# Fillers that follow the token loads, and a second hand-written issue order, in an adaLN block with local attention and a token-mixing MLP

## The chip, the cores and the metric

The kernel runs on one core of a Trainium2 chip. A core has five engines, each with its own instruction queue that is worked off in order: TensorE (PE in the profile, the matrix engine; its weight loads are shown as PEld), VectorE (DVE), ScalarE (ACT), GpSimd (POOL) and SyncE (SP), which here only issues DMA transfers. The engines wait for one another by semaphores. Matrix results land in PSUM, everything else lies in SBUF.

The metric is the time of one execution on the device, in microseconds (us). The kernel before takes 198.67 us, the median of three runs (198.6, 198.67 and 198.73). Smaller is better.

## What is computed

One block of 2048 tokens of 512 features. A vector c gives six modulation rows (shift, scale and gate for two halves). The first half is attention with 32 heads of 16 features, in which each token sees eight tokens: itself and those 2, 4, ... 14 places back. The second half is an MLP that mixes tokens, not features: w1 is 2048 x 1792 and takes the sum over all tokens. Cut to what matters:

```
mod = silu(c) @ w_mod                       # sa, ca, ga, sb, cb, gb
h = layernorm(x) * (1 + ca) + sa
q, k, v = h @ wqkv                          # 32 heads of 16
logits[s, w] = q[s] . k[s - 2w] / 4         # w = 0..7, masked where s - 2w < 0
x = x + ga * (softmax(logits) @ v[s - 2w]) @ wo
h = layernorm(layernorm(x) * (1 + cb) + sb)
u = gelu(einsum("sd,sf->df", h, w1) + b1)   # sum over all 2048 tokens
x = x + gb * (einsum("df,fs->ds", u, w2) + b2).T
```

## The kernel before, in words

Tokens lie in 16 tiles of 128. They are worked in five chunks of 2, 4, 4, 4 and 2 tiles (chunk 0 is tiles 0 and 1, chunk 1 tiles 2 to 5, and so on). Each step of the work is an operation with a name, built by a Python graph (`_Graph.add_any`). Many have alternatives on several engines. The order in which the operations are written out, and so the order of each engine's queue, is a table by hand or by a planner outside the file: the string `ORDER` (line 180 on). A name in it may carry a letter: `:a`, `:d`, `:p` choose ACT, DVE or POOL, `:s` skips the operation, and `:q` writes a matmul as four column tiles of 32 instead of one of 128. Without a letter the first alternative holds. `schedule` also gives out buffers in that order: six PSUM banks (`ps`), four product buffers (`big`), five buffers for shifted v (`vd`).

The names that the change and the prediction speak of:

- `ld_x*`, `ld_wmod*`, `ld_wqkv*`, `ld_wo*`, `ld_w1_*`, `ld_w2_*`, `ld_row*`: loads, issued from SP. `ld_wmod1` and `ld_wmod0` bring the scale and the shift of the first half.
- `ident`, `halo0`, `consts`: constants made on GpSimd. `cps` transposes c; `silu_exp`, `silu_dve` make silu(c); `modcols1` and `modcols0` (line 553 on) are 32 small matmuls that make the scale and the shift as columns; `a1col` and `sab` copy them out of PSUM.
- `ln1s*`, `ln1v*`, `rstd1_*`, `rste1_*`, `nb1_*`, `n1_*`: statistics and normalization of tiles for chunk 0 to 4. Statistics are one pass on DVE or two on ACT (`:a`).
- `tr0_0`, `tr1_0`, `tr1_2` transpose chunks 0 and 1 on PE; `hT0_0` to `hT0_3` and `hT1_*` take them out of PSUM and multiply by `a1col`. The four of chunk 0 read one PSUM bank. Chunks 2 to 4 are transposed by DMA (`xt6` to `xt15`, on SP), and their weights are scaled instead (`wsc0_*`, `wsc1_*`, `wsc2_*`).
- `qvb0`, `qvb1`, `qkv<chunk>_<which><group>`, `ev*`: projections to q (0), k (1) and v (2), and their way out of PSUM.
- `qk*`: the products of q and shifted k, on DVE, into `big`; `red*` sums them over features on PE in column tiles; `max`, `sub`, `exp`, `esum`, `rcp`, `rcq`, `smB` are the softmax. `a2_*` and `vd*` are DMA copies of the weights and of shifted v; `pv*` are the second products on DVE and `pvacc*` their sums on PE, again in column tiles; `oev*` copies them out.
- `wo*`, `x1_*`: output projection and residual. Where `x1_*` runs on ACT, PE adds the residual with a fifth matmul; where it runs on DVE, PE makes four.
- `ln2*`, `n2_*`, `aff*`, `afb*`, `ln3*`, `h3_*`: the two layernorms of the second half, tile by tile. `n2` and `h3` may run on ACT, DVE or GpSimd. `aff` and `afb` of a group of tiles (0, 2, 6, 10, 12, 14, 15) read all the `n2` of the group.
- `mlp1_<part>_<row block>_<first tile>`: the token sum with w1. As soon as some tiles of `h3` are ready, PE can work on their share; partial sums are parked (`park`, `padd`). The weights come through a ring of three buffers (`wst`). `gelu*`, then `mlp2_*` with w2, `fin*` on DVE and the stores `st_out*` from SP or ACT.
- `warm*` (line 523 on): fillers, matmuls on the identity whose result nobody reads. `warm0` is twelve of them, placed by the dependence `wmA1` between `cps` and `modcols`. Seven more blocks of two exist; the table skips six, and `warm1` stands at the very end.

All operations are written by one helper, so every row of the profile has line 131; rows are told apart by their tiles (`big`, `hT`, `wst` and so on).

Of the kernel before, what the change touches and what calls it, by code (L numbers as in the profile page):

```python
# [186 lines left out]
ev0_12 ln1v12 ln1v13 wsc1_1:a qkv0_22 qk0_1 qkv1_13 ld_wmod2 ld_wo3 qk0_0 qk0_2 n1_8 red0_0 red0_1 ln1s11:a qkv1_03:q  # L187
qvb_cp1 qk0_3 xt6 red0_2 ld_wmod3 ev1_13 ev1_03 red0_3 mask wsc2_3:a ln1v11 ln1s10 ld_b1 ld_wo0 xt8 ev0_20 xt7 qkv1_11
ev1_11 ln1v10 max0 qkv1_01 ev1_01 rstd1_3 ev0_22 qk1_3 xt9 sub0 exp0 qkv1_00 ev1_00 qkv1_10 ev1_10 wsc1_0:a vd0_0
qk1_1 qkv1_02 esum0 rcp0 wsc0_2:p qk1_0 ev1_02 qkv1_12 qkv1_23 ld_wmod4 ld_wmod5 rcq0 ev1_12 qkv1_21 rste1_3 smB0  # L190
# [838 lines left out]
```

## Time and profile before

| | |
|---|---|
| runs | 198.6, 198.67, 198.73 us |
| span of the profiled execution | 196.8 us, from its first to its last instruction; no time of its own is listed beside it, the median stands 1.9 above it |
| granted TensorE clock | 0.999 on average |
| PE busy | 185.2 us (94%), 1850 matmuls |
| DVE busy | 156.6 us (80%) |
| ACT busy | 124.9 us (63%) |
| POOL busy | 19.9 us (10%) |
| HBM | 22.03 MB read, 2.10 MB written |

In a row of the profile the numbers after an operation are the count and the busy time or duration; a bracket tells how long the engine stood idle before it, and what ended that. A row in order of time begins with its start and its length. PE rows overlap, since matmuls are pipelined: the pace is read from start to start. The chain that ended last is followed back from the last instruction, each step to what released it.

### The profile page before, as it was taken

The numbers are of one execution on the slowest core, as the hardware profiler recorded it, in microseconds if no ns is written. First come the engines' busy times: TensorE is split into PE (matmuls) and PEld (weight loads), VectorE is DVE, ScalarE is ACT, GpSimd is POOL, SyncE is SP. The second block draws the span as 40 slices with busy tenths as digits, with TensorE's granted clock in tenths as the row PEclk, the third lists the DMA queues.
The fourth block names the chain that finished last, engine by engine and source line by source line (L and its number), as shares of the span: only waits on it lengthen the run. The fifth ranks groups of instructions, "written<-read, shape, count | busy, mean of one in ns | idle before, by whom it ended". The sixth has DMA issues, their size and how long they took to land.

```text
span 196.8 us, 4628 instructions
## 1 busy us (share of the span) xinstructions
PE 185.2 (94%) x1850; PEld 95.5 (48%) x1867; DVE 156.6 (80%) x244; ACT 124.9 (63%) x293; POOL 19.9 (10%) x38
## 2 busy tenths in 40 slices
PE   0699999999999999899999999999999999999994
PEld 0369554654444467244544454444444444444453
DVE  2888999999999999999999999965841633453664
ACT  6877999998999999999797889812760000000000
POOL 5123006320000005030000031200000000000000
PEclk9999999999999999999999999999999999999999
DMA  5998478778899732969674768888939293001112
GB/s 169 312 366 248 115 165 256 235 216 238 165 193 317 252 131 80 312 167 249 199 200 136 159 176 180 197 250 170 336 65 309 82 257 102 30 27 53 53 53 82
DMA packets 55369, 35.95 MB, mean 183 GB/s; under 512 B 24628, under 2 KB 52788, under 8 KB 55348
## 3 DMA queue, kind: packets, MB, share of 16 engines
q1 hardware_dynamic: 53468, 34.05, 63.2%
q10 hardware_dynamic: 1880, 1.61, 2.5%
q8 instruction: 14, 0.23, 0.5%
q14 instruction: 7, 0.06, 0.1%
HBM read 22.03 MB, written 2.10 MB: 123 GB/s over the span
## 4 chain that ended last, share of the span: by engine, by line
PE 73%; DVE 13%; ACT 5%; issue 3%; DMA 2%; SPq 1%; POOL 0%; DVEq 0%; ACTq 0%
PE psS L131 71%; DVE big L131 9%; DVE h L131 2%; PE psL L131 2%; ACT junk L131 1%; SPq L131 1%; DMA vD<-v_sb 1%; ACT xx L131 1%; DMA xx<-in_A_x_dram 1%; DVE m L131 1%; ACT o_sb L131 1%; ACT lsb L131 0%; DVE mv L131 0%; POOL h L131 0%; ACT v_sb L131 0%
## 5 line engine op out<-in xcount | busy, mean ns | idle before, releaser
L131 PEld LDWEIGHTS <-wst 128*128 128x128 bf16 (+1 forms) x566 | 35.5, 100 | 31.9 <-issue 1.3
L131 PE MATMUL psS<-h,wst 128*32 128x512 bf16 (+1 forms) x400 | 50.5, 379 | 0.4 <-issue 0.3
L131 DVE TENSOR_TENSOR big<-q_sb,k_f 128x4096 bf16<-128x4096 bf16 (+1 forms) x20 | 36.4, 1857 | 0.5 <-ACT k_f L131 0.5
L131 DVE TENSOR_TENSOR big<-a2sb,vD 128x4096 bf16<-128x4096 bf16 (+1 forms) x20 | 36.6, 1858 | 0.0
L131 DVE SCALAR_TENSOR_TENSOR h<-psS,bcol,rows_bc 128x512 f32<-128x512 f32 (+2 forms) x18 | 12.4, 690 | 24.2 <-PE psS L131 24.0
L131 PE MATMUL psS<-hT,w_qkv 128*32 128x512 bf16 (+3 forms) x414 | 28.7, 337 | 0.8 <-ACT v_sb L131 0.4
L131 PEld LDWEIGHTS <-w_qkv 128*32 128x32 bf16 (+1 forms) x462 | 19.9, 108 | 16.4 <-issue 2.7
L131 PE MATMUL psS<-gT,big 128*128 128x512 bf16 x109 | 24.3, 379 | 0.2
L131 POOL TENSOR_SCALAR h<-xx,rs,nb 128x512 bf16<-128x512 bf16 x6 | 10.6, 1777 | 84.2 <-DVE nb L131 84.2
L131 PEld LDWEIGHTS <-big 128*128 128x128 bf16 x144 | 12.0, 98 | 13.7 <-issue 0.5
L131 ACT ACTIVATE junk<-xx 128x512 bf16<-128x512 bf16 x28 | 17.7, 631 | 1.3 <-DVE xx L131 0.3
L131 ACT ACTIVATE h<-xx,nb,rs 128x512 bf16<-128x512 bf16 x22 | 17.2, 818 | 0.4 <-DVE nb L131 0.4
L131 PE MATMUL psS<-woq,o_sb 128*32 128x512 bf16 (+1 forms) x123 | 15.8, 380 | 0.4 <-ACT o_sb L131 0.4
L131 ACT ACTIVATE gT<-psS,bcol 128x512 bf16<-128x512 f32 x14 | 8.8, 686 | 10.6 <-DVE psS L131 10.6
L131 DVE TENSOR_TENSOR psS<-psS,gT 128x512 f32<-128x512 f32 x14 | 9.2, 695 | 6.3 <-PE psS L131 6.3
L131 DVE TENSOR_TENSOR h<-h,xx 128x512 bf16<-128x512 f32 (+2 forms) x18 | 11.4, 633 | 0.7
L131 ACT ACTIVATE q_sb<-psS,qvb 128x512 bf16<-128x512 f32 (+1 forms) x20 | 11.6, 603 | 0.3 <-PE psS L131 0.2
L131 PEld LDWEIGHTS <-group 128*32 128x32 bf16 x288 | 7.0, 96 | 9.8 <-issue 4.0
L131 PE MATMUL psS<-hT,wst 128*128 128x256 bf16 (+2 forms) x74 | 11.3, 333 | 0.1
L131 ACT ACTIVATE v_sb<-psS,qvb 128x512 bf16<-128x512 f32 (+1 forms) x20 | 11.2, 607 | 0.0
L131 DVE TENSOR_TENSOR h<-h,rows_bc 128x1024 bf16<-128x1024 bf16 (+2 forms) x14 | 10.5, 759 | 0.0
L131 ACT ACTIVATE k_f<-psS 128x512 bf16<-128x512 f32 x16 | 9.7, 606 | 1.1 <-PE psS L131 1.1
(90 smaller groups left out, 223.3 us busy)
## 6 DMA issues: line engine op xcount, KB each, us to landing
vD<-v_sb SPq DMA_DIRECT2D x12, 524.5 KB, 4.8
big<-in_B_w_dram SPq DMA_DIRECT2D x4, 896.0 KB, 7.5
vD<-v_sb SPq DMA_DIRECT2D x8, 268.5 KB, 3.1
wst<-in_B_w_dram SPq DMA_DIRECT2D x3, 640.0 KB, 5.4
xx<-in_A_x_dram SPq DMA_DIRECT2D x7, 256.0 KB, 5.6
wst<-in_B_w_dram SPq DMA_DIRECT2D x2, 800.0 KB, 4.7
gT<-in_w_mod_dram SPq DMA_DIRECT2D x3, 512.0 KB, 5.4
wst<-in_B_w_dram SPq DMA_DIRECT2D x2, 768.0 KB, 5.6
```

Source lines behind the costliest of these rows:

```text
L131: r = fn(*a, **k)
```

## The change

Two things are changed together.

The fillers: eight blocks of 1, 3, 8, 1, 1, 3, 2 and 1 matmuls (`WARM`). A second tuple, `GATE`, gives five of them a tile of tokens as the moving operand in place of the identity: blocks 2 to 6 multiply tiles 1, 8, 2, 4 and 6, and so cannot run before that tile is loaded. None is skipped. `warm0` loses its place between `cps` and `modcols` (the dependence `wmA1` is gone), and the table places all eight: on PE the order at the beginning becomes `cps`, `warm0`, `warm1`, `warm7`, `warm3`, `warm4`, `warm2`, `warm6`, `modcols1`, `tr0_0`, `warm5`, `modcols0`, `tr1_0`, `tr1_2`, `qvb0`, `qkv0_00`, `qkv0_10`, `qkv0_02`. Before it was `cps`, `tr0_0`, `warm0`, `modcols1`, `modcols0`, `tr1_2`, `tr1_0`, `qvb0`, `qkv0_00`, `qkv0_02`, `qkv0_10`.

The table: the same 805 names in another order, and with other letters at 99 of them. On GpSimd the operations are now `ident`, `halo0`, `consts`, `n1_1`, `n1_0`, `n1_5`, `n1_7`, `n1_6`, `n1_9`, `wsc1_3`, `wsc1_2`, `n1_8`, `n1_10`, `n2_1`, `halo_v2`, `n2_5`, `h3_1`, `h3_0`, `halo_v4`, `n2_8`, `n2_13`, `h3_10`, `h3_13`, `h3_12`; before they were `halo0`, `ident`, `consts`, `n1_0`, `wsc0_1`, `wsc1_2`, `wsc0_3`, `wsc0_2`, `n1_13`, `halo_v2`, `n2_5`, `h3_0`, `h3_1`, `n2_12`, `n2_13`, `n2_15`, `h3_11`. Of the transposes of chunk 0, three of four evacuations go from DVE to ACT, of chunk 1 two of three. `:q` stands at 37 names instead of 48. Written one behind the other, PE's operations change between column-tiled ones (`red`, `pvacc`, `mask`, `modrow` and those with `:q`) and whole ones 26 times before and 16 times now. `esum4` goes from PE to DVE, `x1_10` from ACT to DVE. Behind its last `pvacc4`, PE had `mlp1_0_11_2`, `wo15`, `wo14`, `mlp1_0_13_0`, `mlp1_0_13_2`, `mlp1_0_11_6` and `mlp1_0_13_6` left of the parts before `mlp1_1` (18 matmuls with w1); now it has `mlp1_0_12_6`, `wo14`, `wo15`, `mlp1_0_13_0`, `mlp1_0_13_2` and `mlp1_0_13_6` (14). On SP `vd0_0` now stands between `a2_0_1` and `a2_0_2`, and `ld_w1_1_1408` behind `ld_w1_2_640`, no longer ahead of `ld_w1_2_0`; between `mlp1_1_9_10`, the last reader of the buffer that `ld_w1_2_640` fills, and `mlp1_1_11_10`, which needs `ld_w1_1_1408`, stand 35 matmuls.

```diff
@@ -178,60 +178,60 @@
 ORDER = """
-halo0 ident ld_c act_table cps silu_exp ld_x1 ld_x0 ln1s0 ln1v0 ln1s1:a ln1v1 rstd1_0 rste1_0 ld_x_2_8 ld_x_1_2 nb1_0
-consts ln1s9 silu_dve n1_1 n1_0:p tr0_0 ln1s8 ld_x_1_4 ln1s4:a ld_x_2_6 ln1s3:a warm0 ln1s5 ln1s7 ld_wmod1 ln1v5
-ld_wmod0 modcols1 modcols0 ln1v9 ln1v8 ln1v4 ln1s2 ln1v2 ld_wqkv0 ln1v7 ln1v3 ln1s6 ln1v6 rstd1_1 rste1_1 nb1_1 n1_4:d
-rstd1_2 rste1_2 n1_2:d n1_5:d nb1_2 ld_wqkv1 n1_3 n1_7 n1_6:d a1col hT0_2:d n1_9 tr1_2 tr1_0 hT1_1 wsc0_1:p hT0_1:d
-sab hT0_0:d ld_x_3_12 hT0_3:d hT1_3:d qvb0 qvb_cp0 qkv0_00 warm6:s wsc1_3:a hT1_2:d qkv0_02 ev0_00 ld_wqkv2 qkv0_10
-qkv0_12 ld_b2 ev0_10 ld_x_4_14 wsc1_2:p qkv0_20 wsc0_0 qvb1 ld_x_3_10 wsc0_3:p hT1_0:d ev0_02 wsc2_2:a ln1s13 ln1s12
...
-wo13 ln3s6 vd4_1 ln3v9 ln3v6 ln3s7 wo12 x1_10 ln2m10 ln3v7 mlp1_0_9_0 ln2q11 x1_12:d mlp1_0_9_2 ln2q10 a2_4_0 ln2w10
...
-ld_w1_1_896 h3_11:p mlp1_1_7_10 padd1_7 gelu7 padd1_4 padd1_5 mlp1_1_8_10 mlp1_1_10_10 padd1_10 ld_w1_1_1408 padd1_6
...
-fin15_0 st_out15_0 mlp2_15_2 mlp2_15_1 fin15_2 fin15_1 st_out15_1 st_out15_2:a warm1
+ident halo0 ld_c cps act_table silu_exp silu_dve ld_x1 ln1s1 warm0 ld_x0 ln1s0 ln1v0 ln1v1 rstd1_0 ld_x_2_8 ld_x_1_2
+ld_x_1_4 ld_x_2_6 ld_wmod1 ln1s2 ln1s3 warm1 rste1_0 consts nb1_0 ln1v2 warm7 ln1s8:a ln1s5 ln1v8 ln1v3 ld_wmod0 warm3
+ln1v5 ln1s4 warm4 warm2 ln1s9:a ln1v9 warm6 ln1s7 ln1v4 ld_wqkv0 rstd1_1 modcols1 ln1s6 ld_wqkv1 n1_1:p rste1_1 nb1_1
+n1_0:p n1_4 ln1v7 tr0_0 ln1v6 n1_3:d a1col warm5 modcols0 rstd1_2 n1_2:d n1_5:p tr1_0 rste1_2 nb1_2 ld_x_3_12 ld_wqkv2
+tr1_2 n1_7:p sab qvb0 ld_b2 hT0_3 ld_x_4_14 hT0_1 n1_6:p hT0_0:d ld_x_3_10 hT0_2 ld_wmod2 hT1_2 hT1_1 qkv0_00 wsc1_1:a
+wsc0_2 hT1_0 qkv0_10 qkv0_02 qkv0_12 wsc0_0 ev0_10 hT1_3:d qvb_cp0 ev0_00:d qkv0_20 qkv0_22 ln1s13 ld_wo3 n1_9:p
+wsc0_1:a xt6 ev0_02 ld_wmod5 ln1s12 qkv1_03 qk0_0 qvb1 ev0_12 wsc1_0:a wsc1_3:p qkv1_13 qk0_1 red0_0 qk0_3 red0_1
...
+qkv1_00 ln1s10:a ln1v15 ev0_20 ev1_11 n1_8:p ln1v13 qk1_3 ln1v11 xt8 xt7 qkv1_10 qkv1_23 xt9 max0 ln1v10 sub0 ev1_01
...
+qkv1_20 a2_0_2 a2_0_0 rste1_4 ld_wo2 vd0_2 halo_v1:a ev1_22 vd0_3 biascols sub1 vd0_1 ev1_21 qkv2_03 pv0_0 pvacc0_0
...
+qkv3_13 ev3_02 n2_1:p aff0 xt14 pv1_0 ev3_11 qkv3_00 halo_v2 afb0 ev3_01 pv1_1 sub2 exp2 pvacc1_0 ev3_00 oev1_0
...
+qk4_2 ln2q7 ln2q8 mlp1_0_1_2:q red4_2 mlp1_0_3_0:q vd3_1 ln2m6 park0_1 qk4_3 pv3_0 mlp1_0_2_2:q ln2w6 halo_v4 rstd2_6
...
+mlp1_0_6_0:q oev3_0 mlp1_0_7_2:q mlp1_0_6_2:q pvacc3_2 n2_8:p mlp1_0_5_0:q mlp1_0_5_2:q oev3_2 pvacc3_1 max4 pv3_3
...
+esum4:d rcp4 ld_w1_0_1408 wo13 park0_6 wo12 afb6 rcq4 x1_13:d smB4 wo11 a2_4_2 wo10 x1_12:d x1_11:d ln3s7:a ln3s9:a
+ln3s6 ln3s8 mlp1_0_11_0 ln3v7 mlp1_0_9_0 ln3v6 ln2q11 ln3v8 mlp1_0_9_2 ln3v9 vd4_3 mlp1_0_11_2 x1_10:d rstd3_6 rste3_6
...
+ld_w1_1_1408 padd2_1 mlp1_2_2_11 mlp1_2_0_11 mlp1_2_0_14 ld_w2_7 gelu7 ld_w2_5 gelu1 mlp1_2_4_11 mlp1_2_4_14 padd2_4
...
+st_out15_0:a st_out15_1:a mlp2_15_2 fin15_2 st_out15_2:a st_out14_0
 """
...
     INJ=(),
-    WARM=(12, 2, 2, 2, 2, 2, 2, 2),
+    WARM=(1, 3, 8, 1, 1, 3, 2, 1),
+    GATE=(None, None, 1, 8, 2, 4, 6, None),
 ):
     nc = _OrderedNC(tc, 1)
     G = _Graph(dict(ps=6, big=NBIG, vd=NVD))
@@ -522,20 +523,18 @@
 
     for w_, n_w in enumerate(WARM):
         s_w = _Slot("ps")
-
-        def f_warm(s_w=s_w, n_w=n_w):
+        g_w = GATE[w_]
+
+        def f_warm(s_w=s_w, n_w=n_w, g_w=g_w):
+            rhs = _ap(ident[:, 0:1], [[0, 4], [1, P]]) if g_w is None else xx[:, g_w, :]
             for _ in range(n_w):
-                nc.tensor.matmul(ps(s_w), lhsT=ident[:], rhs=_ap(ident[:, 0:1], [[0, 4], [1, P]]), start=True, stop=True)
-        if w_ == 0:
-            f_warm0, s_w0 = f_warm, s_w
-            continue
-        G.add_any([("pe", 0.216 * n_w, f_warm), ("skip", 0.0, lambda: None)], reads=["ident"], alloc=s_w, frees=s_w,
-                  name=f"warm{w_}")
+                nc.tensor.matmul(ps(s_w), lhsT=ident[:], rhs=rhs, start=True, stop=True)
+        G.add_any([("pe", 0.216 * n_w, f_warm), ("skip", 0.0, lambda: None)],
+                  reads=["ident"] + ([] if g_w is None else [("xx", g_w)]), alloc=s_w, frees=s_w, name=f"warm{w_}")
 
     s_c, s_m = _Slot("ps"), (_Slot("ps"), _Slot("ps"))
     add("pe", 0.18, lambda: nc.tensor.matmul(ps(s_c)[:, 0:KT], lhsT=c_t[:], rhs=ident[0:KT, 0:KT], start=True,
                                              stop=True), reads=["c_t", "ident"], alloc=s_c, name="cps")
-    add("pe", 0.216 * WARM[0], f_warm0, after=[G.ops[-1]], alloc=s_w0, frees=s_w0, writes=["wmA1"], name="warm0")
     add("act", 0.2, lambda: nc.scalar.activation(ecol[:], ps(s_c)[:, 0:KT], ACT.Exp, scale=-1.0), reads=[s_c, "act_table"],
         writes=["ecol"], name="silu_exp")
 
@@ -550,10 +549,10 @@
             for kt in range(KT):
                 nc.tensor.matmul(ps(s_m[v])[:, dt_:dt_ + 1], lhsT=wmodA[:, kt, v * D + dt_ * P: v * D + (dt_ + 1) * P],
                                  rhs=sc[:, kt:kt + 1], start=(kt == 0), stop=(kt == KT - 1))
-    add("pe", 0.42, lambda: f_cols(1), reads=["sc", ("wmodA", 1), "wmA1"], writes=["wmA1"], alloc=s_m[1], name="modcols1")
+    add("pe", 0.42, lambda: f_cols(1), reads=["sc", ("wmodA", 1)], alloc=s_m[1], name="modcols1")
     add("dve", 0.15, lambda: nc.vector.tensor_scalar_add(a1col[:], ps(s_m[1])[:, 0:KT], 1.0), frees=s_m[1],
         writes=["a1col"], name="a1col")
-    add("pe", 0.42, lambda: f_cols(0), reads=["sc", ("wmodA", 0), "wmA1"], frees=s_wm, alloc=s_m[0], name="modcols0")
+    add("pe", 0.42, lambda: f_cols(0), reads=["sc", ("wmodA", 0)], frees=s_wm, alloc=s_m[0], name="modcols0")
     add("dve", 0.15, lambda: nc.vector.tensor_copy(sab[:], ps(s_m[0])[:, 0:KT]), frees=s_m[0], writes=["sab"],
         name="sab")
     scale_w(1)
```

More of the change, by code (lines that the diff above doesn't have):

```diff
@@ L186 @@
-qkv0_12 ld_b2 ev0_10 ld_x_4_14 wsc1_2:p qkv0_20 wsc0_0 qvb1 ld_x_3_10 wsc0_3:p hT1_0:d ev0_02 wsc2_2:a ln1s13 ln1s12
[L187 to L190, printed above, removed]
@@ L211 @@
-mlp1_0_7_0:q pv3_2 pvacc3_0 mlp1_0_5_2:q oev3_0 esum4:q nb2_6 n2_7 mlp1_0_6_2:q warm7:s rcp4 pv3_1 n2_6 park0_5 pv3_3
-n2_9 pvacc3_2 n2_8 aff6 oev3_2 mlp1_0_7_2:q rcq4 pvacc3_1 oev3_1 mlp1_0_8_2:q smB4 ld_w1_0_1152 mlp1_0_10_0:q
-ld_w1_0_1408 pvacc3_3 vd4_2 mlp1_0_10_2 vd4_0 warm2:s park0_6 oev3_3 wo11 afb6 x1_11:d a2_4_3 ln3s8 ln3v8 ln3s9:a wo10
-wo13 ln3s6 vd4_1 ln3v9 ln3v6 ln3s7 wo12 x1_10 ln2m10 ln3v7 mlp1_0_9_0 ln2q11 x1_12:d mlp1_0_9_2 ln2q10 a2_4_0 ln2w10
-rstd3_6 rste3_6 nb3_6 a2_4_2 h3_6:d h3_7:d mlp1_0_12_0 mlp1_0_12_2 h3_8:d rstd2_10 h3_9 mlp1_0_7_6 mlp1_0_8_6 ln2q12
```

75 lines of the change are left out of this document (38 added, 37 removed).

## The prediction, made before the result was known

> **What bounds the kernel now.** First the engines' busy time by stage (start:end and length in us; busy us of PE, PEld, DVE, ACT, POOL).
>
> ```profile
> 18.07:112.00 93.93, 91.69 (x1230) 48.10 (x1238) 93.53 (x107) 88.43 (x213) 10.62 (x5) 1.00 0.74 199
> 125.70:190.70 65.00, 64.68 (x298) 29.48 (x302) 33.69 (x51) 10.94 (x16) 0.00 (x0) 1.00 0.51 141
> ```
>
> From 18.07 to 112 us VectorE (DVE) stands still 0.40 us, TensorE (PE) 2.24: the two are bound together. After 125.7 the matrix engine works alone. Then the chain that ended last:
>
> ```profile
> 6.47 10.88 PE psS L131 x108
> 18.07 1.79 DVE big L131 x2
> 82.77 7.30 PE psS L131 x33
> 184.29 6.44 PE psS L131 x29
> 194.23 0.29 DVE h L131
> ```
>
> It is PE until the first product (DVE big, 18.07), DVE in the stretch after it, PE again from 82.77 to 190.73, and 6.1 us of last outputs. So the time is: when qkv0 and the first product begin, plus the work of the slower of two engines, plus a fixed end. How the beginning is made (PE and DVE in order of time):
>
> ```profile
> 2.20 0.18 PE L131 MATMUL psS<-ident,c_t 4*128 4x4 bf16 x1 [2.20 <-DMA c_t<-in_c_dram]
> 6.47 1.03 PE L131 MATMUL psS<-ident,h 128*128 128x128 bf16 x8 [4.09 <-POOL h L131]
> 7.30 5.20 PE L131 MATMUL psS<-ident 128*128 128x512 bf16 x12
> 12.33 0.94 PE L131 MATMUL psS<-sc,big 128*128 128x1 bf16 x32
> 13.13 1.05 PE L131 MATMUL psS<-ident,h 128*128 128x128 bf16 x16
> 14.02 0.67 PE L131 MATMUL psS<-sab,wst 128*128 128x1 bf16 x16
> 14.55 3.66 PE L131 MATMUL psS<-hT,wst 128*128 128x256 bf16 x32
> 12.90 0.16 DVE L131 TENSOR_SCALAR a1col<-psS 128x4 f32<-128x4 f32 x1 [0.59 <-PE psS L131]
> 18.07 1.23 DVE L131 TENSOR_TENSOR big<-q_sb,k_f 128x2048 bf16<-128x2048 bf16 x1 [0.51 <-ACT k_f L131]
> ```
>
> tr0 waits for GpSimd's n1_0; behind it stand the twelve fillers, 0.42 us each ((12.33-7.30)/12), and only then modcols, whose scale a1col every hT needs. Transposes go at 0.104 us at 6.47 and 0.056 at 13.13: the matrix clock opened after about 5.8 us of work. Landings of w_mod, w_qkv (rows of the tiles big and wst) and the fifth token load:
>
> ```profile
> L131 SPq DMA_DIRECT2D big<-in_w_mod_dram x2: 470/488/505, 3.7 to 4.2; - x2
> DMA to landing us min/median/max: 6.0/6.0/6.0
> L131 SPq DMA_DIRECT2D wst<-in_A_wqkv_dram x2: 507/753/999, 4.8 to 5.3; - x2
> DMA to landing us min/median/max: 7.8/8.3/8.8
> 6.66 0.63 ACT L131 ACTIVATE junk<-xx 128x512 bf16<-128x512 bf16 x1 [0.28 <-DMA xx<-in_A_x_dram]
> ```
>
> w_mod's first half is there at 3.7+6.0 = 9.7 us and is used at 12.33. The wqkv halves land at 12.6 and 14.1; token loads 3 and 4 land before 6.6 (an estimate: 6.0 for the fourth).
>
> **Part 1, the head.** Five fillers now follow cps at 2.4: 5 x 0.42, to 4.5. One waits for tile 8, two for tile 2 (6.0 to 6.85), eight follow (their tile 1 is long there), two wait for tile 6. With 5.8 us from 2.4 to 6.0 the clock opens between 8.2 and 11.8; at 9.5, six of the eight go at half clock, the rest and the last two at 0.22: end 10.3. modcols1 takes 0.8 (12.33 to 13.13): 11.1. On DVE silu_dve goes first, in the 3.5 us in which DVE waits for the first tokens (below), and a1col now stands behind eight statistics passes instead of seven:
>
> ```profile
> L131 DVE BATCH_NORM_STATS2 st<-xx 128x6 f32<-128x512 bf16 x10 | 6.7, 684 | 3.5 <-DMA xx<-in_A_x_dram 3.5
> L131 ACT ACTIVATE v_sb<-psS,qvb 128x256 bf16<-128x256 f32 x8 | 3.4, 486 | 0.0
> L131 ACT ACTIVATE h<-xx,nb,rs 128x512 bf16<-128x512 bf16 x22 | 17.2, 818 | 0.4 <-DVE nb L131 0.4
> ```
>
> Six after tile 2 is there: 6.0 + 6 x 0.67 + small ones 0.9 = 10.9, nb1_1 and n1_3 to 11.6; a1col at 11.7 instead of 12.90. ACT does n1_4 (0.82) and rstd1_2, then three of the four hT0 evacuations from 12.15 at 0.43 (3.4/8, the nearest PSUM-to-SBUF row) one behind another: 13.45. PE: tr1 from 12.25 (n1_2 and n1_5), two blocks of 0.45 to 13.2, qvb0 0.55, so qkv0_00 at 13.75 instead of 14.55: **-0.8**. Bounds: -1.35 (wqkv0 at 12.6, qvb0 behind it) and +0.2, if the clock opens at 11.8 only. ACT then has two hT1, wsc1_1, hT1_0 ahead of ev0_10: 13.45 + 4 x 0.62 = 16.0, ev0_10 0.6, first product at 16.65 instead of 18.07: **-1.4 on DVE**; the second q/k matmul block moved up (qkv0_10 behind qkv0_00) is part of that.
>
> **Part 2, fewer mode changes.** PE runs column-tiled (128*32) and whole work in turn; each change costs.
>
> ```profile
> 66.69 0.38 PE L131 MATMUL psS<-xx,ident 128*128 128x512 bf16 x1
> 67.00 1.05 PE L131 MATMUL psS<-woq,o_sb 128*32 128x512 bf16 x16
> 67.87 0.39 PE L131 MATMUL psS<-xx,ident 128*32 128x512 bf16 x4
> 83.42 0.38 PE L131 MATMUL psS<-xx,ident 128*128 128x512 bf16 x1
> 83.64 1.03 PE L131 MATMUL psS<-woq,o_sb 128*128 128x512 bf16 x4
> ```
>
> Whole to whole 0.22 (83.42 to 83.64), whole to tiled 0.31 (66.69 to 67.00): 0.09 a change. Four tiled groups take 0.87 (67.00 to 67.87), as whole ones do: a :q itself costs nothing. By the tables the changes go from 26 to 16: **-0.9 on PE**; bounds 0 (changes that fall into a wait) and -0.9.
>
> **Part 3, operations that change engine.** x1_10 goes to DVE, so wo10 drops its residual matmul: -0.2 on PE. esum4 goes to DVE: -0.2 on PE. On DVE between the first product and pv4's last:
>
> ```profile
> L131 DVE TENSOR_REDUCE m<-psL 128x64 bf16<-128x512 f32 x2 | 1.3, 671 | 0.0
> L131 DVE SCALAR_TENSOR_TENSOR xx<-psS,xx 128x512 bf16<-128x512 f32 x5 | 3.4, 684 | 0.1
> L131 DVE TENSOR_SCALAR h<-h,mv,rs 128x512 bf16<-128x512 bf16 x9 | 3.2, 404 | 0.0
> ```
>
> esum4 +0.67, x1_10 +0.68 and a read +0.08, one h3 less -0.40, ln3s7 to ACT -0.68: +0.35. ACT loses some seven n1 passes (0.82 each) to GpSimd and gains hT passes; it has 5.5 us to spare in the long stretch, so nothing.
>
> **Part 4, queues.** SP: vd0_0 now stands between the a2_0 copies, so the last of four comes one issue (0.61) later:
>
> ```profile
> L131 SPq DMA_DIRECT2D a2sb<-lsb x4: 609/612/733, 31.3 to 33.4; - x4
> DMA to landing us min/median/max: 2.5/2.9/3.4
> 36.91 1.22 DVE big L131
> ```
>
> Last landing now 33.4+2.5 = 35.9 at the earliest, 36.7 at the most, pv0 at 36.91: with 0.61 more, 0 to 0.4 late; I take 0.15. Moved loads (wst, w2, token and row loads) I cost at nothing: the cover is PE work of 7.5 us between freeing and use, 35 matmuls, for ld_w1_1_1408 (now behind ld_w1_2_640); landing as late as w_qkv's slower half (8.8) it would cost 1.3. The outputs' queues change only where 6.1 us of end are fixed by DVE. The final filler is gone; it stood behind the last product.
>
> GpSimd (POOL): n1_1, n1_0, n1_5, n1_7, n1_6, n1_9, two wsc, n1_8 in a row, before the first product; n1_10, n2_1, n2_8, halo_v4 beside DVE.
>
> ```profile
> 5.64 0.77 POOL L131 TENSOR_SCALAR h<-xx,rs,nb 128x512 bf16<-128x512 bf16 x1 [2.11 <-DVE nb L131]
> 31.42 4.91 POOL L131 TENSOR_SCALAR h<-xx,rs,nb 128x512 bf16<-128x512 bf16 x1 [15.17 <-DVE nb L131]
> 75.80 2.67 POOL L131 TENSOR_SCALAR h<-xx,rs,nb 128x512 bf16<-128x512 bf16 x1 [33.58 <-DVE nb L131]
> ```
>
> Alone 0.77; beside products 2.67 and 4.91, and DVE shows no idle there. n2_1 and n2_8 are awaited by aff0 and aff6, behind a maximum on DVE: 0 to 0.77 each, taken 0.15 each, since 75.80 was hidden. n1_8 feeds xt8, which blocks SP; if it misses the gap before the products (16.2 against 16.65) it comes after four of them, at 22, with SP free at 28.4 for smB0 at 29.5: hidden.
>
> [...]
>
> **The sum.** PE: -0.8 -0.9 -0.4 = -2.1. DVE up to pv4: -1.4 +0.35 +0.15 +0.3 = -0.6; behind pv4's last product PE has four mlp1 matmuls less left (14 against 18, at 0.216): -0.86, so -1.5. The later one decides: -1.5, which I round towards nothing, **-1.4**, for the load of w1 above. The profiled span is 196.8, so 195.4; the runs' median stands 1.9 above the span, so 198.67-1.4 = **197.3 us**.
>
> **Rivals.** [...]
> C, the fillers do not open the clock earlier: they stand ahead of modcols1 in PE's order, and 18 at 0.42 end at 11.1, modcols1 at half clock; qkv0 +0.2 instead of -0.8, the product -0.4 instead of -1.4: DVE side -0.5, 198.2. For it: the 5.8 us of the trace, from tile 2's landing on. [...]
> D, the tables do not fit: with longer whole runs PE and DVE wait for one another at each tiled run. The nearest rows:
>
> ```profile
> 81.22 0.61 PE L131 MATMUL psS<-big,group 128*32 128x512 bf16 x8 [0.52 <-DVE big L131]
> 82.77 0.82 PE L131 MATMUL psS<-woq,o_sb 128*128 128x512 bf16 x3 [0.37 <-ACT o_sb L131]
> ```
>
> Eight tiled runs at 0.52 are 4.2 against 2.24 idle now: +2.0, 199.3. Against it: DVE's work decides there and is not longer.
>
> **Chances.** A (197.3; by itself 196.3 to 198.2) 0.56, B 0.12, C 0.10, D 0.22. 0.2% (0.4 us) is about what a measurement tells from no change. Faster: A and half of C, 0.61; same: part of C and the low edge of D, 0.06; slower: B and D, 0.33. The range reaches from A's low end to D: 196.2 to 199.5, leaving B and A's far edge out.
>
> **What would show it.** Right: qkv0 near 13.75 and the first product near 16.65; fillers from 2.4 and modcols1 by 11; 16 changes; PE from pv4 on without gaps. Wrong: DVE products longer than 2.28 us or idle before aff0 and aff6 (B); fillers at 0.42 to the end (C); PE idle over 2.24 us between the first product and 112, or the first product early and the lead gone by wo14 (D).

## The result and the profile after

The changed kernel takes 197.3 us, the median of four runs (196.78 to 197.62), beside 198.63 us for the kernel before (198.35 to 198.73): a ratio of 0.9932 with a 95% interval of 0.9907 to 0.9957. The predicted time was 197.3 us, and the direction is right. Both traces together show that the number came out right in part by luck: the lead at the head was larger than its term, what DVE loses behind it was larger too, and a part of the gain lies outside the profiled span. The ratios here and below are the record's estimates, not quotients of medians, and leave out the executions that took over 1.5% more than the fastest of their kernel (three with five fillers, one with the fillers alone).

The stages of the changed kernel, in the columns of the first fence of the prediction (start:end, length, busy us of PE, PEld, DVE, ACT, POOL; then granted clock, DMA share, GB/s):

```profile
18.07:112.00 93.93, 91.05 (x1152) 47.40 (x1158) 93.25 (x108) 87.61 (x210) 10.25 (x8) 1.00 0.68 193
114.50:143.90 29.40, 29.08 (x147) 13.22 (x142) 24.20 (x58) 20.05 (x47) 3.07 (x4) 1.00 0.97 272
125.70:190.00 64.30, 63.92 (x295) 29.31 (x300) 34.59 (x53) 11.78 (x20) 1.53 (x2) 1.00 0.45 132
```

As before, DVE has next to no idle time up to 112 us (0.68 us) and PE has none that matters behind it. Five pieces of the chain that ended last:

```profile
9.76 9.20 PE psS L131 x124
32.23 0.77 POOL h L131
101.72 0.94 DVE psS L131
126.38 10.52 PE psS L131 x48
180.12 12.55 PE psS L131 x85
```

The chain no longer runs through the fillers: it comes to 9.76 from the landing of w_mod. New links are a GpSimd operation at 32.23 and `esum4` on DVE at 101.72. From 126 us on PE works in one piece, so the moved loads of w1 cost nothing. The head, in order of time:

```profile
2.31 2.31 PE L131 MATMUL psS<-ident 128*128 128x512 bf16 x5
5.69 3.25 PE L131 MATMUL psS<-xx,ident 128*128 128x512 bf16 x11 [0.39 <-DMA xx<-in_A_x_dram]
9.76 0.55 PE L131 MATMUL psS<-sc,big 128*128 128x1 bf16 x16 [0.82 <-DMA big<-in_w_mod_dram]
11.67 1.05 PE L131 MATMUL psS<-ident,h 128*128 128x128 bf16 x16
13.22 3.78 PE L131 MATMUL psS<-hT,wst 128*128 128x256 bf16 x32
10.68 0.15 DVE L131 TENSOR_SCALAR a1col<-psS 128x4 f32<-128x4 f32 x1
16.27 4.62 DVE L131 TENSOR_TENSOR big<-q_sb,k_f 128x2048 bf16<-128x2048 bf16 x4
```

Eleven fillers took 3.25 us, not 4.7: most ran at 0.22 us, not 0.43, since the matrix clock opened at about 7.2 (the packed trace lists full clock from 7.16, that of the kernel before from 12.23). `modcols1` begins at 9.76 instead of 12.33, qkv0 at 13.22 instead of 14.55, the first product at 16.27 instead of 18.07.

How this lead goes on is read from six points of each trace (us; starts of the first three, then the ends of the last product of `pv0` and `pv4`, the start of the last `mlp1` matmul, the end of DVE's last operation, and the span):

| | modcols1 | qkv0 | first product | pv0 end | pv4 end | last mlp1 | DVE end | span |
|---|---|---|---|---|---|---|---|---|
| before | 12.33 | 14.55 | 18.07 | 41.52 | 114.84 | 145.01 | 194.52 | 196.84 |
| changed | 9.76 | 13.22 | 16.27 | 40.87 | 114.51 | 143.86 | 193.37 | 195.69 |
| difference | -2.57 | -1.33 | -1.80 | -0.65 | -0.33 | -1.15 | -1.15 | -1.15 |

Of 1.80 us on DVE, 0.33 is left at the end of `pv4`. Then 0.82 is won behind it, where PE alone decides. Between first product and end of `pv4` DVE needs 98.24 us instead of 96.77, 1.47 more. By groups of its instructions: `esum4` +0.93, `x1_10` with its read +0.71, the products of q and k +0.35, the small statistics operations +0.33, waits +0.28, the statistics pass gone to ACT -0.64, one `h3` less -0.23; the other groups, all small, make -0.26 together.

### The profile page after: what moved, and what is told of

It reads as the page before. It is cut to its first block, busy times and chain, and to the rows that moved or that the text cites. A ratio compares the mean times of both kernels' runs of the same rounds, so it can differ in the third digit from the quotient of the medians.

```text
span 195.7 us, 4366 instructions
## 1 busy us (share of the span) xinstructions
PE 185.7 (95%) x1716; PEld 95.1 (49%) x1732; DVE 158.0 (81%) x243; ACT 123.6 (63%) x291; POOL 22.8 (12%) x45
## 4 chain that ended last, share of the span: by engine, by line
PE 48%; DVE 18%; issue 15%; DMA 9%; ACT 4%; SPq 4%; POOL 1%; DVEq 0%; POOLq 0%; ACTq 0%
PE psS L131 47%; DVE big L131 9%; DVE h L131 4%; SPq L131 4%; DMA big<-in_w_mod_dram 3%; DMA hT<-h 3%; DMA w_qkv<-in_B_w_dram 2%; ACT junk L131 1%; DVE xx L131 1%; DVE st L131 1%; PE psL L131 1%; DMA a2sb<-lsb 1%; DVE mv L131 1%; DVE m L131 1%; ACT xx L131 1%
## 5 line engine op out<-in xcount | busy, mean ns | idle before, releaser
L131 DVE TENSOR_TENSOR big<-q_sb,k_f 128x4096 bf16<-128x4096 bf16 (+1 forms) x20 | 37.0, 1877 | 0.3 <-ACT k_f L131 0.3
L131 PE MATMUL psS<-gT,big 128*128 128x512 bf16 x110 | 24.9, 379 | 0.1
L131 POOL TENSOR_SCALAR h<-xx,rs,nb 128x512 bf16<-128x512 bf16 x12 | 13.3, 1116 | 92.5 <-DVE nb L131 87.2
L131 ACT ACTIVATE junk<-xx 128x512 bf16<-128x512 bf16 x26 | 16.3, 627 | 0.4
L131 PE MATMUL psS<-woq,o_sb 128*128 128x512 bf16 (+1 forms) x75 | 15.6, 379 | 0.1
L131 ACT ACTIVATE h<-xx,nb,rs 128x512 bf16<-128x512 bf16 x15 | 12.0, 810 | 2.1 <-DVE nb L131 2.1
L131 PE MATMUL psS<-big,group 128*32 128x512 bf16 (+1 forms) x160 | 10.1, 338 | 2.0 <-DVE big L131 1.5
L131 ACT ACTIVATE v_sb<-psS,qvb 128x512 bf16<-128x512 f32 (+1 forms) x20 | 11.2, 601 | 0.2 <-PE psS L131 0.2
L131 ACT ACTIVATE q_sb<-psS,qvb 128x512 bf16<-128x512 f32 (+1 forms) x18 | 10.7, 622 | 0.1
```

The costliest lines, as they stand in the source:

```text
L131: r = fn(*a, **k)
```

## Experiments

The twelve kernels ran in groups of four; each group shared a chip and the runs of the kernel before, whose median was 198.39, 198.32 and 198.34 us in the three. The ratios are against those runs.

The traces are compared at the points of the table above, for two things at the end of an execution blur the medians, and no row shows their cause. Behind DVE's last operation the span runs on for 2.32 to 2.34 us, but for 2.61 to 2.72 us in three kernels (the new head alone, the new rest alone, `n1_10` on ScalarE), where by the packed trace one closing instruction comes 0.3 us late. And the time lies beyond the span by 1.7 us (medians 1.70 to 1.74) in all ten sets of runs with the new order behind the first product, but by 2.0 us (1.95 to 2.03) in the kernel before and two others with its order, and by 2.2 us in the new head alone. So some 0.25 us of the changed kernel's gain come with the new order and lie outside the span.

### Without the fillers

```diff
-warm0 warm1 warm7 warm3 warm4 warm2 warm6 warm5
+warm0:s warm1:s warm7:s warm3:s warm4:s warm2:s warm6:s warm5:s
```

> The changed kernel with all eight filler blocks skipped; its table and everything else stay. Theory: the fillers open the matrix clock (full pace at 7.2 us in the changed kernel, 12.2 before), so without them PE's first work is modcols1 at 9.76, the clock opens some 3.4 to 6 us later, tr, qvb and the first qkv0 blocks go at half pace, qkv0 starts near 14.2 instead of 13.2 and its 48 matmuls of 256 columns lose up to 0.11 each: the first product 1.5 to 3 us later, and the time 198.5 to 200. Rival: the earlier start comes from the order of DVE, ACT and GpSimd alone, and PE has time at the beginning: within 0.3 us of the changed kernel, 197.0 to 197.6.

Measured: 198.84 us (197.4 to 200.1), ratio 1.0017 (0.9991 to 1.0043). The first product began at 17.18, `pv4` ended at 115.44. PE in the head:

```profile
8.97 0.58 PE L131 MATMUL psS<-sc,big 128*128 128x1 bf16 x16 [6.59 <-DMA big<-in_w_mod_dram]
11.51 1.89 PE L131 MATMUL psS<-ident,h 128*128 128x128 bf16 x16 [0.53 <-DVE h L131]
13.76 2.46 PE L131 MATMUL psS<-hT,wst 128*128 128x256 bf16 x16
```

The profiled execution took 198.33 us. `modcols1` is even earlier, but sixteen transposes take 1.89 us instead of 1.05 and the first sixteen matmuls of qkv0 2.46: about half the pace (transposes at 0.105 us, against 0.056 in the prediction's rows), until the clock opened at 14.92, 5.95 us after `modcols1` began. That is the late end of the 3.4 to 6 us expected; the early end is shown only once, as 3.41 us at half clock with the fillers alone (below). The time is the theory's: without the fillers this order has no gain left, and by these rows it is the earlier clock that they bring.

### The new head alone, and the new rest alone

The order is cut at `qk0_0`, the first product. One kernel has the changed table ahead of it and the old order and letters behind it; the other has the old head with its twelve fillers and the changed order behind.

```diff
# new head, old rest
-halo0 ident ld_c ... (before, up to qk0_0)
+ident halo0 ld_c cps ... warm6 modcols1 ... (changed, up to qk0_0)
# old head, new rest
-qk0_0 qk0_2 n1_8 red0_0 ... (before, from qk0_0 on)
+qk0_0 qvb1 ev0_12 wsc1_0:a ... (changed, from qk0_0 on)
```

> The new fillers and the new table up to the first product (everything that stands ahead of qk0_0), then all other operations in the old order with the old letters. Theory: the head alone brings 1.3 us on PE and 1.8 on DVE, and the old rest, whose DVE has less to do up to the last pv4, keeps it: 196.8 to 197.4, the changed kernel's time or a little less. Rival (the new rest is what brings it, by 16 changes of mode instead of 26): 198 to 198.6.

> The old fillers and the old table up to its first product, then all other operations in the new order with the new letters. Theory: DVE does 1.4 us more between the first product and the last pv4 in the new order, PE has 0.86 less left behind it: 0.4 to 0.8 us slower than before, 199.0 to 199.4. Rival (PE decides, ten changes of mode fewer, 0.9, and two matmul groups fewer, 0.4): 197.3 to 197.8.

Measured: the head alone 198.58 us, ratio 1.0008 (0.999 to 1.0027); the rest alone 200.25 us, ratio 1.0075 (1.005 to 1.01). For the rest alone the time is 0.85 us above the theory's band. For the head alone the theory missed and the rival's number came. Its fillers, in a profiled execution that took 198.93 us, above the median:

```profile
5.84 4.85 PE L131 MATMUL psS<-xx,ident 128*128 128x512 bf16 x11 [0.72 <-DMA xx<-in_A_x_dram]
10.49 0.61 PE L131 MATMUL psS<-sc,big 128*128 128x1 bf16 x16
```

With the same beginning the eleven fillers now took 4.85 us at 0.43 each, and `modcols1` waited for them, not for w_mod. The first product came 0.94 earlier instead of 1.80. Of that, 0.41 is left at the end of `pv4`, and nothing is added behind it: from there to the last `mlp1` it is 30.17 us, as before, against 29.35 in the changed kernel. In the rest alone it is 29.35 too, so the 0.82 belongs to the new rest, whatever head stands before it (four matmuls fewer at 0.216 us would be 0.86; no run takes them alone). In time not even the 0.41 of the head alone is seen, since its end is longer, as told above. The rest alone loses 2.17 us up to the end of `pv4`; two of DVE's waits:

```profile
24.01 2.29 DVE L131 TENSOR_TENSOR big<-q_sb,k_f 128x4096 bf16<-128x4096 bf16 x1 [0.59 <-ACT k_f L131]
112.10 1.22 DVE L131 TENSOR_TENSOR big<-a2sb,vD 128x2048 bf16<-128x2048 bf16 x1 [0.93 <-DMA a2sb<-lsb]
```

The parts do not add up: -0.4 and +1.35 at DVE's end apart, -1.15 together. From first product to `pv4` DVE waits 1.91 us in the rest alone, 0.40 in the kernel before and 0.68 in the changed one. The wait at 24.01 fits a new rest that asks for results earlier than the old head delivers them; why the one at 112.10 grew (0.26 us in the changed kernel) is not shown. The old rest gives half of the new head's lead back, most of it in two waits of DVE (0.20 and 0.28 us).

### esum4 and x1_10 back from DVE

```diff
-esum4:d ... x1_10:d
+esum4:q ... x1_10
```

> The changed kernel with esum4 back on PE (column-tiled) and x1_10 back on ACT, with the fifth matmul of wo10. Theory: DVE decides up to pv4; it loses 0.94 and 0.77 us there, PE gains 0.4 of work: faster than the changed kernel by 0.5 to 1.3, 196.0 to 196.8. Rival: PE decides: 0.2 to 0.4 slower, 197.5 to 197.7.

Measured: 197.95 us, ratio 0.9981 (0.996 to 1.0003), slower than the changed kernel; the rival is nearer, though 0.25 us too low. The theory fell: 1.6 us of work left DVE, and its waits rose from 0.68 to 2.55 us. (With `esum4` column-tiled PE has 18 mode changes, not 16.)

```profile
37.77 1.23 DVE L131 TENSOR_TENSOR big<-a2sb,vD 128x2048 bf16<-128x2048 bf16 x1 [0.85 <-DMA vD<-v_sb]
104.18 0.69 DVE L131 SCALAR_TENSOR_TENSOR xx<-psS,xx 128x512 bf16<-128x512 f32 x1 [0.75 <-PE psS L131]
108.72 0.16 DVE L131 SCALAR_TENSOR_TENSOR nb<-mv,rs 128x4 f32<-128x4 f32 x1 [0.60 <-ACT rs L131]
```

The second and third stand where the two operations had been: without them DVE waits for PE and ACT. So `esum4` and `x1_10` on DVE fill its waits and cost little. The first came because `pv0` was reached 0.5 us sooner than in the first profile of the changed kernel (35.70 against 36.19) while `vd0_2`, the copy it waits for, landed 1.0 later (37.68 against 36.70). That points at SP's queue, where this copy stands behind `ld_wo2`.

### The changed kernel again, and three edits of it

```diff
# n1_10 on ScalarE
-n1_10:p
+n1_10
# copies first: the a2_0 copies together, the vd0 copies ahead of ld_wo2
-a2_0_1 ... vd0_0 ... a2_0_2 a2_0_0 rste1_4 ld_wo2 vd0_2 ... vd0_3 ... vd0_1 ev1_21
+a2_0_1 a2_0_2 a2_0_0 ... vd0_0 ... rste1_4 vd0_2 ... vd0_3 ... vd0_1 ld_wo2 ev1_21
# five fillers in warm2
-    WARM=(1, 3, 8, 1, 1, 3, 2, 1),
+    WARM=(1, 3, 5, 1, 1, 3, 2, 1),
```

> The changed kernel once more, beside the next three. Theory (the moment at which the matrix clock opens moves from one execution to the next): 196.8 to 197.7 us, and the profile has modcols1 anywhere between 9.7 and 10.5 us, with qkv0 0.6 to 0.8 us behind its place in the first profile if the fillers go at 0.43 us up to modcols1. Rival (the opening follows from the program): fillers change from 0.43 to 0.22 us near 7 us again, modcols1 at 9.8, qkv0 at 13.2.

> The changed kernel with n1_10 on ScalarE instead of GpSimd. [...]

> The changed kernel with the four a2_0 copies one behind another and the four vd0 copies ahead of the load ld_wo2. Theory (SP's order in the changed table holds pv0 when the head is early, as in the run with the two operations put back): pv0's last product ends 0.2 to 0.8 us earlier against the same head, and the time falls by 0.2 to 0.6 us against the changed kernel run beside it. Rival (in the changed kernel DVE is not idle before pv0, so the copies are hidden): within 0.2 us of it.

> The changed kernel with warm2 of five matmuls instead of eight. Theory (the eighteen fillers hold modcols1 when the clock opens late): modcols1 waits only for w_mod, at 9.7 us whatever the clock does, so the time is 0 to 0.4 us less than that of the changed kernel beside it. Rival (with a pause of 0.5 us or more ahead of modcols1 the clock opens later): matmuls at half speed into qkv0, first product at 17 or later, 0.5 to 1.5 us more.

| | median, us | ratio (interval) | modcols1 | first product | pv0 end | pv4 end | DVE end | span |
|---|---|---|---|---|---|---|---|---|
| changed again | 197.17 | 0.9943 (0.9926 to 0.996) | 10.14 | 16.48 | 40.71 | 114.36 | 193.20 | 195.54 |
| n1_10 on ScalarE | 197.74 | 0.9974 (0.9957 to 0.999) | 10.07 | 16.41 | 40.75 | 114.47 | 193.31 | 196.03 |
| copies first | 196.88 | 0.9933 (0.9911 to 0.9955) | 9.91 | 16.28 | 40.18 | 113.97 | 192.81 | 195.15 |
| five fillers | 197.25 | 0.9945 (0.9921 to 0.9969) | 9.96 | 16.27 | 40.50 | 114.26 | 193.11 | 195.44 |

The first result repeats. The fillers were at 0.22 us by 7 again, as the rival had it; `modcols1` is later because w_mod landed later, and its range is the one that the theory gave:

```profile
5.94 2.77 PE L131 MATMUL psS<-xx,ident 128*128 128x512 bf16 x11 [0.19 <-DMA xx<-in_A_x_dram]
10.14 0.55 PE L131 MATMUL psS<-sc,big 128*128 128x1 bf16 x16 [1.43 <-DMA big<-in_w_mod_dram]
```

What GpSimd does to DVE is seen by laying the first profile of the changed kernel beside the second. First:

```profile
32.23 0.77 POOL L131 TENSOR_SCALAR h<-xx,rs,nb 128x512 bf16<-128x512 bf16 x1 [15.85 <-DVE nb L131]
32.39 2.75 DVE L131 TENSOR_TENSOR big<-q_sb,k_f 128x4096 bf16<-128x4096 bf16 x1 [0.33 <-ACT k_f L131]
```

Second:

```profile
32.37 2.29 DVE L131 TENSOR_TENSOR big<-q_sb,k_f 128x4096 bf16<-128x4096 bf16 x1
32.59 2.71 POOL L131 TENSOR_SCALAR h<-xx,rs,nb 128x512 bf16<-128x512 bf16 x1 [15.90 <-DVE nb L131]
```

In this pair the operation that starts first is not stretched: GpSimd's `n1_10` takes 0.77 us when it begins 0.16 ahead of the product, and the product then takes 2.75 instead of 2.29; when it begins 0.22 behind, it takes 2.71 itself. DVE had waited 0.33 us for `k_f` there, which let GpSimd in. In no other of the fourteen profiles did DVE lose as much (0.15 us at most). Beside the second profile, moving `n1_10` to ScalarE therefore had nothing to win: the 0.3 to 0.5 us that the author had expected from a product at 2.29 us again did not come, and no longer wait for `k_f` ahead of it either. DVE's end moved by 0.11 us, and the other 0.4 of the span lie behind the last output, 0.3 of it in one gap between two closing instructions of GpSimd. Why is open.

The copies: `pv0`'s first two products in the second profile, and then with the copies first.

```profile
35.71 1.22 DVE L131 TENSOR_TENSOR big<-a2sb,vD 128x2048 bf16<-128x2048 bf16 x1
37.14 1.23 DVE L131 TENSOR_TENSOR big<-a2sb,vD 128x2048 bf16<-128x2048 bf16 x1 [0.21 <-DMA vD<-v_sb]
```

```profile
35.49 2.35 DVE L131 TENSOR_TENSOR big<-a2sb,vD 128x2048 bf16<-128x2048 bf16 x2
```

The wait is gone, and from the first product to `pv0`'s end it is 23.90 us instead of 24.23. The median, 0.29 us lower, lies in the expected band, but the two intervals overlap: the trace shows the mechanism, the runs do not resolve its size. It is the fastest kernel of the study.

Five fillers: `modcols1` waited for w_mod alone, as the theory had it, and the median did not move. But four of its twelve runs took 198.9 to 200.3 us, the other eight 196.8 to 197.4, while all twelve of the changed kernel beside it lie between 196.7 and 197.9. So in some executions the time rose by even more than the rival had said (1.7 to 3.1 us above the median of the changed kernel). No trace of these was taken, but the three longest list a mean granted clock of 0.981 to 0.983, the fourth and the other eight 1.0.

### Mode changes, added where PE decides and taken away where DVE does

```diff
# added: ten blocks behind pv4 in nine runs (the first two have no whole block between them)
-mlp1_1_0_10 mlp1_1_6_10 mlp1_1_4_10 mlp1_1_3_10 mlp1_1_10_10
-mlp1_1_9_10 mlp1_2_3_14 mlp1_2_1_14 mlp1_2_0_11 mlp1_2_4_11
+mlp1_1_0_10:q mlp1_1_6_10:q mlp1_1_4_10:q mlp1_1_3_10:q mlp1_1_10_10:q
+mlp1_1_9_10:q mlp1_2_3_14:q mlp1_2_1_14:q mlp1_2_0_11:q mlp1_2_4_11:q
# taken away, in the kernel before
-qkv2_03 ... esum2 ... qkv4_00 ... sub3 ... qkv3_22
+qkv2_03:q ... esum2:q ... qkv4_00:q ... sub3:q ... qkv3_22:q
```

> The changed kernel with ten mlp1 blocks of the stretch behind pv4 column-tiled, each between whole ones: 18 mode changes more, where the matrix engine alone decides. Theory (a change costs 0.09 us wherever nothing covers it): 18 x 0.09 = 1.6 us more than the changed kernel, 198.5 to 199.1 us. Rival (a change is free, and the 0.31 us of the quoted rows is something else): within 0.3 us of it, 197.0 to 197.5.

> The kernel before with qkv2_03, esum2, qkv4_00, sub3 and qkv3_22 column-tiled: 16 mode changes instead of 26, all of them ahead of pv4, nothing else touched. The prediction's term, taken in full: 0.9 us less, 197.4 to 197.7. The theory now (ahead of pv4 VectorE decides, and what the matrix engine saves there it waits): within 0.3 us of the kernel before, its idle time between the first product and 112 us up from 2.24 by 0.5 to 0.9 us.

Measured: with 18 changes added 199.32 us, a little above the theory's band, ratio 1.0047 (1.003 to 1.0063); with ten fewer in the kernel before 198.35 us, ratio 1.0004 (0.9986 to 1.0021). The added ones, from `pv4`'s end to the last `mlp1` (in the changed kernel this is the second row of the first fence above):

```profile
114.90:146.00 31.10, 31.10 (x224) 12.04 (x220) 24.22 (x57) 20.04 (x47) 3.05 (x4) 1.00 0.92 258
```

By the points of the traces the stretch takes 31.11 us (114.85 to 145.96) instead of 29.35: 1.76/18 = 0.098 us a change, if four column tiles cost what a whole matmul does, as the prediction's rows show. The price of the prediction, 0.09, is right, and it is paid where nothing covers it. The medians lie 2.15 us apart; in the profile `pv4` also ends 0.49 later than in the changed kernel run again.

Taken away ahead of `pv4`, changes bring nothing. `pv4` ended at 114.68 instead of 114.84. What became of the 0.9 us is seen in PEld's waits from 18.07 to 112 us (total, times, longest), in the kernel before, in this one and in the changed kernel:

```profile
PEld L131 <- DVE big L131: 1.5, 2, 1.0
```

```profile
PEld L131 <- DVE big L131: 2.2, 2, 1.6
```

```profile
PEld L131 <- DVE big L131: 4.3, 6, 1.2
```

PE comes to the products earlier and waits for them longer. The second part of the expectation missed: the matrix engine's own idle time did not rise but fell, from 2.24 to 1.84 us (93.93 less its busy time), though the part of it that waits for products rose from 0.7 to 1.4:

```profile
18.07:112.00 93.93, 92.09 (x1318) 49.36 (x1316) 93.58 (x107) 88.60 (x214) 10.42 (x5) 1.00 0.73 200
```

The waits listed with PEld (2.2 us) are longer than those of PE itself (1.4), and PE's busy time rose by 0.40 us; PE's idle time alone is a poor gauge here.

### DVE relieved, on top of the copies

```diff
 (copies first, as above)
-esum4:d  qkv2_12 qkv2_02 qkv2_22 wo0 wo1  qkv3_10 qkv3_01 qkv3_13 qkv3_00 sub2  qkv3_12 qkv3_03 qkv4_10 wo3 wo5 wo4
+esum4:q  (each of the sixteen others, three runs of whole blocks, with :q)
```

> The changed kernel with the copies first, esum4 back on the matrix engine and three more whole blocks column-tiled (12 mode changes instead of 16), to beat both kernels. Theory (VectorE decides up to pv4): 0.9 us of VectorE's work gone, of which waits give back up to half; 196.2 to 196.6 us. Rival (the two engines are as long as one another there, so VectorE waits as much as it saves): 196.8 to 197.4 us, VectorE's idle time up from 0.5 to 1.2 us or more.

Measured: 197.2 us (196.55 to 197.97), ratio 0.9929 (0.9904 to 0.9954). The rival's time came: DVE's work lost the 0.93 us of `esum4`, its waits between first product and `pv4` rose from 0.47 to 1.02 (1.2 had been expected), some small operations grew, and from first product to DVE's end it took 176.48 us against 176.53 with the copies alone. The largest wait:

```profile
103.36 0.69 DVE L131 SCALAR_TENSOR_TENSOR xx<-psS,xx 128x512 bf16<-128x512 f32 x1 [0.67 <-PE psS L131]
```

### The fillers alone

The kernel before with the eight filler blocks, and `tr0_0` behind `modcols1`:

```diff
-cps ... tr0_0 ... warm0 ... modcols1 modcols0
+cps warm0 warm1 warm7 ... warm3 warm4 warm2 warm6 modcols1 tr0_0 warm5 modcols0
```

> The kernel before with the eight filler blocks of the changed one in place of its twelve matmuls, and tr0_0 behind modcols1; the rest of the table as before. Theory (the fillers bring modcols1 forward, but DVE's old order has a1col behind seven statistics passes, and the old order of the evacuations holds qkv0): modcols1 at 9.8 to 10.5, qkv0 0.2 to 0.8 us sooner, 197.5 to 198.1 us. Rival (the fillers alone bring the whole 1.3 us of the head): qkv0 at 13.2 to 13.5, 197.0 to 197.4 us. Second rival (nothing): 198.2 to 198.6.

Measured: 199.13 us, ratio 1.0012 (0.9984 to 1.004). The twelve runs fall apart: five took 197.72 to 198.31 us, near the theory, and seven 199.04 to 201.02, above all three. One of the seven was profiled (199.71), and it shows a reason that none of the three named:

```profile
5.88 2.53 PE L131 MATMUL psS<-xx,ident 128*128 128x512 bf16 x11 [0.70 <-DMA xx<-in_A_x_dram]
9.83 0.55 PE L131 MATMUL psS<-sc,big 128*128 128x1 bf16 x16 [1.41 <-DVE mv L131]
11.74 2.09 PE L131 MATMUL psS<-ident,h 128*128 128x128 bf16 x16
18.31 3.50 DVE L131 TENSOR_TENSOR big<-q_sb,k_f 128x2048 bf16<-128x2048 bf16 x3 [1.27 <-ACT k_f L131]
```

The clock opened at once (eleven fillers in 2.53 us), PE then stood still for 1.41 us, and the transposes at 11.74 are at half clock again (2.09 us). The granted clock, the third column from the end, shows it in three stretches:

```profile
8.64:12.05 3.41, 2.13 (x44) 1.62 (x45) 3.34 (x17) 2.62 (x10) 0.00 (x0) 1.00 1.08 370
12.05:15.46 3.41, 3.41 (x38) 3.02 (x39) 2.84 (x12) 2.65 (x4) 1.87 (x3) 0.50 1.10 351
15.46:18.40 2.94, 2.94 (x29) 2.93 (x28) 1.64 (x6) 1.62 (x4) 0.94 (x2) 1.00 1.03 309
```

qkv0 began 0.37 earlier than before, went more slowly, and the first product began 0.24 later. The mean granted clock of this execution is 0.991. Of the other six long ones one lists 0.991 too and the longest 0.983; the other four list 0.998 to 1.0, and what held them is not shown.

## Why the prediction was right, and where it was not

- **The head (part 1).** The mechanism held: without fillers the gain is gone. The sizes were off. The clock was taken to open at 9.5, with bounds of 8.2 and 11.8. In the traces with the new fillers the pace changes anywhere from 5.2 us (the fillers alone) to 11.2 (the new head alone), which the bounds did not allow on the early side. `modcols1` began at 9.76 to 10.5, where the fillers had been taken to end at 10.3 (11.1 was its end). The working counts one filler too many: one matmul waits for tile 2, not two, and 17 stand ahead of `modcols1`, not 18. `a1col` came at 10.68 in the first profile, not 11.7, since DVE was through its statistics sooner. With the whole new head, qkv0 began 0.58 to 1.33 earlier (predicted 0.8; 0.72 to 1.33 with the changed order behind it too), the first product 1.37 to 1.80 (predicted 1.4; with the old rest 0.94).
- **Mode changes (part 2).** The step that failed is "-0.9 on PE" as a gain: 0.09 a change is right (0.098 measured), but ahead of `pv4` PE's time is not the time that decides, and nothing came of it. That did not spoil the total, since the sum took the later of the two engines, and DVE was the later.
- **Operations that change engine (part 3).** DVE was to get 0.35 us of work; the terms named there measured `esum4` 0.93 (taken as 0.67, from a smaller reduction), `x1_10` 0.71 (0.76), one `h3` less -0.23 (-0.40), `ln3s7` -0.64 (-0.68): 0.77. Small statistics operations, which weren't counted, added 0.33, and the waits 0.28. With the two operations taken off, waits took their place, so these terms are not a cost that can simply be had back. "ACT nothing" held but for the 0.33 us at 32.39, once.
- **Queues (part 4).** `pv0` late by 0.15, bounds 0 to 0.4: the place is right, but the copy that is late is `vd0_2`, behind `ld_wo2`, not the last of `a2_0`. The wait is 0 in the first profile, which reached `pv0` late by the collision at 32 us, 0.21 in the second and up to 0.85 in other runs with this order. `n2_1` and `n2_8`, taken at 0.15 each, show no wait of DVE. The operation that cost something was `n1_10` (0.46 us), which the sum had not counted. The loads of w1 cost nothing, as predicted.
- **The sum.** On DVE -1.80 at the start and +1.47 behind it, where -1.4 and +0.8 (0.35, 0.15 and 0.3) had been summed to -0.6; -0.33 came, and -0.48 in the second profile. Behind `pv4` -0.82 and -0.84 came where four matmuls had been put at -0.86. That makes -1.15 and -1.32 instead of -1.5, rounded to -1.4. What the span did not give, the end did: the runs lie 1.7 us above their spans, not the 1.9 that the sum took as fixed (2.0 by the runs of the kernel before that list a span). So the agreement to 0.1 us is luck: an end taken as fixed made up for a gain of the span that had been put too high.
- **The rivals.** B (longer products on DVE, beside GpSimd): in the first profile one product beside `n1_10` was 0.46 us longer, where four operations at 0.77 had been the author's estimate; elsewhere DVE lost 0.15 us at most. No run shows what lengthens the later of two such operations. C: its mechanism occurred in three profiles (the head alone, the two operations back, DVE relieved), as a loss of up to 0.7 us at `modcols1`; in the two profiles of the changed kernel itself it did not occur. D: both its signs came in the first profile. PE's idle time was 2.88 us (93.93 less 91.05), over the 2.24 named, though only 2.08 in the second, whose trace lists twelve matmuls more there (1164 against 1152); and of the lead of 1.80 only 0.33 was left at the end of `pv4`. But what used the lead up was DVE's work, not waiting: DVE's waits grew by 0.28 of the 1.47. PEld's waits for products rose from 1.5 to 4.3 us, while PE had the time that the mode changes saved, and D's loss of 0.6 us did not come.

## What to carry to other kernels

Where two engines are both full, what one saves can be a wait for the other (with 1.6 us of work taken off DVE its waits rose from 0.68 to 2.55): price a saving on the engine that decides in that stretch, and test it by putting the cost where that engine is alone (0.098 us a mode change behind `pv4`, nothing ahead of it). A lead at the head and an order behind it belong together: here neither half was faster alone, and both together were. A pause in the fillers can cost them their effect: in one pair of traces, with 0.57 instead of 0.39 us of waiting for tokens, the clock opened 3 us later (10.25 instead of 7.16), and in one it closed again behind a pause of 1.41 us ahead of `modcols1`, though behind 1.43 and 1.82 us in two others it did not. And a time is more than its last engine: the end of the execution, which had been taken as fixed, was worth some 0.25 us.

## What had not been expected of the hardware

The moment at which the matrix clock opens can be read in one way that fits all fourteen traces. In the trace that shows it closing, the steps of the granted clock lie 3.41 us apart or twice that, and in each of the fourteen the packed trace lists full clock for a whole number of 3.413 us (2 and then 54 of them in this trace, 53 to 56 in the others). Cutting each trace into stretches of 3.41 us that end where the clock opens (its first record, and the change of pace), and taking PE's busy time in the stretch before the change and in the one before that: the clock opened behind every stretch with 2.94 us or more, and behind none with 2.81 or less, 86% and 82% of the stretch. The pair on either side of the border, the first profile of the changed kernel and the run with the two operations back:

```profile
3.75:7.16 3.41, 2.94 (x8) 0.81 (x6) 2.80 (x9) 1.87 (x7) 0.04 (x1) 1.00 0.99 308
```

```profile
3.42:6.84 3.42, 2.81 (x7) 0.81 (x6) 2.65 (x7) 1.58 (x5) 0.12 (x1) 1.00 0.99 311
```

(The granted clock is printed as 1.00 ahead of its first record; the pace of the fillers tells the state.) In the first the fillers went at 0.22 us from 7.2 on. In the second eleven of them took 4.71 us, and `modcols1` began at 10.36. By this reading the pauses in which fillers wait for tokens, 0.1 to 0.7 us ahead of the opening in these traces, decide by their length and place whether the clock opens a stretch earlier or later. It was read from these traces and not tested on others, and fillers that wait for nothing were not tried in this head. Closing has been seen once, with the fillers alone at 12.05, behind a stretch with 2.13 us of busy time, about half of it matmuls with one column. Busy time alone does not tell when it closes, for in the run with changes added the clock stayed open behind a stretch with less:

```profile
6.48:9.89 3.41, 2.03 (x10) 0.69 (x7) 3.24 (x12) 2.34 (x7) 1.52 (x2) 1.00 1.03 341
```

That closing also makes the three longest executions with five fillers is an inference, but their granted clock fits: one stretch at half clock is 0.009 of a span of 197 us and gave 0.991 in the trace, and two stretches would give 0.983 (an estimate), where 0.981 to 0.983 is listed.

Second, DVE lost against GpSimd, by 0.46 us in the pair of rows at 32 us. It lost less in other places: 0.04 to 0.07 us on the first product in five other profiles (1.29 us for 1.22 at most), and 0.15 us on a normalization of `h` near 117 us in eight (0.56 us for 0.41), each time with GpSimd first. In both profiles of that pair the operation that began later was the longer one, and by a little less than the other still had to run: GpSimd had 0.61 us still to run when the product began (0.77 less 0.16), and the product lost 0.46, 0.15 less. The other way round it is much the same: the product had 2.07 us still to run (2.29 less 0.22), and GpSimd lost 1.94 (2.71 less 0.77), 0.13 less. The first products lost 0.15 less than the 0.19 to 0.22 us that GpSimd still had to run. On the normalization, by the first profile, the rest is larger: it began with 0.42 us of GpSimd's operation still to run (117.32 plus 0.77, less 117.67), and lost 0.27 less. No row shows where this rest comes from.
